# Four plain second-layer products instead of two ahead of a pair's outputs, and a later landing time told to a planner

## The chip, the core and the metric

The kernel runs on one core of one Trainium2 chip. The metric is device time in microseconds (us) of one execution, taken as the median of the runs. Five engines work beside each other, each through its own list of instructions in order: PE (matrix products), DVE, ACT and POOL (elementwise work) and SP, which here only issues DMA transfers. They wait for each other through semaphores.

## The reference, cut to what matters

Two blocks follow each other. The first is a chunked state-space scan over 4 sequences of 768 tokens with 8 heads of width 32 and a state of 16:

```
for each chunk:
    L = exp(cum_i - cum_j), lower triangle          # decays inside the chunk
    y = (C B^T * L) x  +  exp(cum) * (C state)      # outputs
    state = exp(cum_last) * state + sum_j exp(cum_last - cum_j) B_j x_j
```

The second is a mixture of 4 experts with a hidden layer of 1024, over the 3072 tokens (width 256) that the first block puts out; p is `domain_probs` divided by its row sum:

```
out = sum_e  p[:, e] * (max(x @ w1[e], 0) @ w2[e])
```

All of it is in float32.

## The kernel before, in words

**Chunks and pairs.** The kernel cuts the tokens into 24 chunks of 128, numbered so that chunks 0 to 3 open the four sequences, 4 to 7 are the second chunks, and so on. Chunks go in pairs. Of a pair, three steps matter here. `decays(c)` (L799) makes the decay triangle of a chunk: for chunks 3 to 5 by two running products on DVE (`scan`, L519) over a tile `ab` of 512 KB that a DMA (`load_decays`, L461, issued at L463) spreads over all partitions; chunk 2 is scanned from PSUM banks instead. There are two `ab` tiles, so chunk 3 and chunk 5 share `ab0`. `scores(cs)` (L844) is 16 small PE products (L502 in the trace) into four PSUM banks, each followed by one DVE multiplication with the triangle (L856) that gives the masked scores `MT`. `outputs(cs)` (L865) is 16 PE products for a pair (32 records of L546, and for chunks 4 and later also products with the carried state at L879); they read `MT`, so they need all four L856 of their pair. ACT then copies the results out (L894, L556), and `carry(c)` (L901) turns the new state on DVE (L910, L912).

**Experts.** A hidden piece of 256 columns is numbered `fb` 0 to 15. Tokens of the first pair go through pieces 0 to 3 plainly: `plain_first(fb)` (L1235) is four matrix instructions into a bank, and `gated` (L965, DVE instruction at L968) takes the bank through max(., 0) and the gate into an SBUF tile. The second layer of these four pieces is the list `own_` (L1390): eight products, two for each piece, all summed in one bank. Every product is two matrix instructions of 128x256 in the program (L933), and each of those is two records in the trace, so a product is four records. Products 1 and 2 need the gated tile of piece 0, 3 and 4 that of piece 1, and so on. All later pairs go through schemes with fewer products and more additions; `token_sums` (L1033, instruction L1043) makes sums of token tiles for them, `operands` (L989, L1024) sums of weights, on POOL or DVE, stored to DRAM at L1029. `twos_begun` (L1075) and the list `ones` (L1401) are first-layer products and two second-layer products of the first such group.

**The order on PE** is written by hand, as a list `line` (L1367 to L1505). Around the change it is: plain first layer of pieces 0 and 1, `scores([2, 3])`, plain first layer of pieces 2 and 3, the first `OWN` products of `own_`, `outputs([2, 3])`, the products of `own_` from `OWN` to `SCORED`, `scores([4, 5])`, the four products of `twos_begun` for both groups, then what is left of `ones` and `own_`, of which the last `LEFT` stand behind `outputs([4, 5])`, and then products on token sums (tiles `Y`).

```
    line.extend(own_[:OWN])
    outputs([2, 3])
...
    fill = own_[OWN:SCORED] + put(*[begun[two][0] for two in twos]) + ones + own_[SCORED:]
    line.extend(fill[:SCORED - OWN])
    scores([4, 5])
    line.extend(fill[SCORED - OWN:len(fill) - LEFT])
    outputs([4, 5])
    line.extend(fill[len(fill) - LEFT:])
```

**The order on the other engines** is made when the program is built, by `Plan.run` (L180): it walks through an assumed clock, in which every piece of work has an assumed duration, and gives an engine that is free the ready work with the earliest due time; due times come from the PE list. It also picks the PSUM bank or SBUF tile that a value lives in. [...] A tile that is filled ahead of the plan is handed over with the time at which the plan may count on it (`plan.taken`, L768 to L782); `now` is 13.2 (L745). That order is fixed in the program. On the chip an engine goes through its list, and an instruction that has to wait holds up everything behind it on that engine.

Of the kernel before, what the change touches and what calls it, by code (L numbers as in the profile page):

```python
# [33 lines left out]
LEAN = 4.0  # L34
EASY = 40.0
SCANNED = 6
SCORED, OWN, LEAD, LEFT = 5, 2, 5, 3
FILLED = 3
HORIZON, OPENING, LOADED = 26.0, 80.0, 1.0
ORDERS = (0, 1, 2, 3), (3, 1, 2, 0), (0, 1, 2, 3), (3, 1, 2, 0)  # L40
# [319 lines left out]
def kernel(  # L360
# [86 lines left out]
    st = {c: {} for c in range(NCH)}  # L447
# [294 lines left out]
    plan = Plan(homes)  # L742
    line = []
    B512, B256 = {"DVE": D512, "POOL": 1.3}, {"DVE": D256, "POOL": .72}
    now = 13.2  # L745
# [28 lines left out]
    for c, i in ((2, 2), (3, 3)):  # L774
        st[c]["xb"] = plan.taken("xb", i, now)
    st[2]["ctm"] = plan.taken("ctm", 0, now)
    st[3]["ab"] = plan.taken("ab", 0, now + 2)
    for c in range(2):
        st[c]["A"] = plan.taken("A", c, now)
    g0 = gates[0, 0] = plan.taken("gate", 0, now)  # L780
# [783 lines left out]
```

## Time and profile before

| what | us |
|---|---|
| runs before | 616.87, 616.92, 619.20; median 616.92 |
| profiled execution, first to last instruction (its span) | 615.3 |
| what lies around the span (median less span) | 1.6 |
| PE busy in the span | 605.7 (98%) |
| DVE, ACT, POOL busy | 489.5, 292.5, 157.6 |
| PE idle ahead of L546 (outputs of chunks 2 and 3) | 1.36 and 0.70 |

Times inside the execution are counted from its first instruction. The time of the profiled execution is its span and the start and end around it; set beside the median of the runs that rest is 1.6 us. "Busy" of PE counts a matrix instruction from its start to its modelled end, and neighbours overlap; so the spacing of two starts, not the duration of one, says how fast PE goes. The granted clock is the share of its full speed that PE was allowed in a stretch.

### The profile page before, as it was taken

What the parts mean: (1) busy time and instruction counts of PE and PEld (TensorE: products, weight loads), DVE (VectorE), ACT (ScalarE), POOL (GpSimd) and SP (SyncE); (2) the same over time, 40 slices, a digit from 0 to 9 for tenths busy, and PEclk for the clock granted to TensorE, in tenths of its full rate; (3) what the DMA queues carried; (4) which work ended last, traced back from release to release, by engine and by line L of the source; (5) the groups of instructions that cost most, each with busy time, mean ns of one, the idle gap of its engine ahead of it and who ended that gap; (6) DMA issues with size and microseconds to landing.
All of it is one profiled execution on the core that took longest, in us unless ns stands there. A gap on an engine that the chain in (4) does not pass through costs nothing.

```text
span 615.3 us, 10136 instructions
## 1 busy us (share of the span) xinstructions
PE 605.7 (98%) x3365; PEld 514.8 (84%) x3365; DVE 489.5 (80%) x854; ACT 292.5 (48%) x681; POOL 157.6 (26%) x238
## 2 busy tenths in 40 slices
PE   9899999999999999999999999999999999999997
PEld 5677878888888888888888888888888888888885
DVE  7879897998969895697978988386785979576775
ACT  4237646378651327877443333844444242434441
POOL 5536556636372000776500100210000000000000
PEclk9899999999999999999999999999999999999999
DMA  7737578676863429983442424964233232964001
GB/s 249 256 114 231 204 218 300 205 224 208 280 188 94 134 34 285 297 291 146 132 144 77 137 63 118 284 222 137 61 111 87 93 90 51 303 230 126 1 0 52
DMA packets 89060, 99.65 MB, mean 162 GB/s; under 512 B 27428, under 2 KB 58928, under 8 KB 89008
## 3 DMA queue, kind: packets, MB, share of 16 engines
q1 hardware_dynamic: 88852, 98.95, 51.4%
q8 instruction: 27, 0.44, 0.3%
q14 instruction: 25, 0.20, 0.1%
q10 hardware_dynamic: 156, 0.06, 0.0%
HBM read 78.80 MB, written 20.17 MB: 161 GB/s over the span
## 4 chain that ended last, share of the span: by engine, by line
PE 92%; DVE 2%; ACT 1%; issue 0%; DVEq 0%
PE bank L933 88%; PE bank L546 2%; PE bank L502 1%; PE bank L879 1%; DVE v L960 1%; DVE v L968 1%; ACT A L556 1%; DVE MT L856 0%; ACT v L894 0%; DVE bank L1071 0%; DVE v L1260 0%; PE bank L1325 0%; DVE v L1425 0%; ACT LT L894 0%; ACT v L1330 0%
## 5 line engine op out<-in xcount | busy, mean ns | idle before, releaser
L933 PE MATMUL bank<-v,w 128*128 128x256 f32 x1716 | 402.0, 381 | 1.1 <-DVE bank L1071 0.8
L933 PEld LDWEIGHTS bank<-v,w 128*128 128x128 f32 x1716 | 325.7, 191 | 50.0 <-issue 2.9
L933 PE MATMUL bank<-Y,w 128*128 128x256 f32 x692 | 177.3, 381 | 0.7 <-ACT LT L894 0.4
L933 PEld LDWEIGHTS bank<-Y,w 128*128 128x128 f32 x692 | 130.2, 190 | 21.9 <-issue 1.7
L1213 ACT COPY v<-bank 128x512 f32<-128x512 f32 x109 | 63.9, 586 | 177.5 <-PE bank L933 165.2
L968 DVE SCALAR_TENSOR_TENSOR v<-bank,gate 128x512 f32<-128x512 f32 x147 | 101.0, 688 | 39.6 <-PE bank L933 36.8
L960 DVE TENSOR_TENSOR v<-v,v 128x512 f32<-128x512 f32 x179 | 125.9, 720 | 2.1 <-ACT v L942 0.8
L1024 POOL TENSOR_TENSOR w<-w,w 128x256 f32<-128x256 f32 x94 | 72.1, 784 | 46.0 <-DVE v L960 13.8
L1071 DVE TENSOR_TENSOR bank<-bank,v 128x512 f32<-128x512 f32 x81 | 55.5, 696 | 35.2 <-PE bank L933 23.6
L942 ACT COPY v<-bank 128x512 f32<-128x512 f32 x97 | 56.7, 587 | 55.0 <-PE bank L933 46.7
L947 ACT COPY bank<-v 128x512 f32<-128x512 f32 x126 | 73.2, 594 | 10.8 <-DVE v L968 8.7
L526 ACT ACTIVATE MT<-ab,neg 128x128 f32<-128x128 f32 x144 | 46.9, 393 | 2.0 <-DMA ab<-cum_d 2.0
L933 PE MATMUL bank<-LT,w 128*128 128x256 f32 x168 | 42.6, 380 | 0.0
L531 POOL TENSOR_SCALAR_AFFINE_SELECT MT<-MT 128x512 f32<-128x512 f32 x36 | 23.0, 652 | 67.8 <-ACT MT L526 53.9
L933 PEld LDWEIGHTS bank<-LT,w 128*128 128x128 f32 x168 | 31.8, 190 | 4.6 <-DVE v L968 0.3
L1024 POOL TENSOR_TENSOR w<-w 128x256 f32<-128x256 f32 x32 | 24.2, 762 | 23.2 <-DVE Y L1043 9.0
L960 DVE TENSOR_TENSOR v<-bank,v 128x512 f32<-128x512 f32 x26 | 17.9, 689 | 11.7 <-PE bank L933 9.9
L1260 DVE TENSOR_TENSOR v<-v,v 128x256 f32<-128x256 f32 x58 | 22.9, 431 | 1.1 <-ACT v L1213 0.7
L856 DVE TENSOR_TENSOR MT<-bank,MT 128x512 f32<-128x512 f32 x36 | 22.7, 681 | 0.1
L968 DVE SCALAR_TENSOR_TENSOR v<-v,gate 128x512 f32<-128x512 f32 x26 | 19.7, 758 | 0.4
L1213 ACT COPY LT<-bank 128x512 f32<-128x512 f32 x12 | 7.0, 586 | 23.5 <-PE bank L933 23.5
L840 POOL TENSOR_TENSOR cts<-ctm,dec 128x256 f32<-128x256 f32 x20 | 14.5, 734 | 11.6 <-DVE v L960 5.1
(110 smaller groups left out, 322.1 us busy)
## 6 DMA issues: line engine op xcount, KB each, us to landing
w<-w_d SPq DMA_DIRECT2D x128, 256.0 KB
w_d<-w SPq DMA_DIRECT2D x64, 256.0 KB
w<-in_w_dram SPq DMA_DIRECT2D x40, 256.0 KB
ab<-cum_d SPq DMA_DIRECT2D x18, 512.0 KB
w<-in_w_dram SPq DMA_DIRECT2D x64, 128.0 KB
gate<-p_d SPq DMA_DIRECT2D x15, 384.0 KB
xb<-in_xbc_dram SPq DMA_DIRECT2D x17, 192.0 KB
out_dram<-v SPq DMA_DIRECT2D x144, 16.0 KB
```

Of the source, the lines that this page charges most:

```text
L526: nc.scalar.activation(out=MT[:, place(c, h), 0:P], in_=ab[:, h * P:h * P + P], func=AF.Exp, bias=neg[:, h % NT, NQ * real(c) + h // NT:NQ ...
L531: nc.gpsimd.affine_select(out=MT[:, h:h + n, 0:P], in_=MT[:, h:h + n, 0:P], compare_op=ALU.is_ge, fill=0.0, base=0, pattern=[[0, n], [1, P ...
L856: nc.vector.tensor_mul(to, g, LT0[:, js, h] if cs[0] < SCANNED else to)
L933: nc.tensor.matmul(out=o, lhsT=w[:, j], rhs=x if half is None else x[:, j], start=(start and j == 0), stop=(j == 1), skip_group_check=True)
L942: act(.5, lambda e: nc.scalar.copy(out=flat(v), in_=bank.t), reads=[bank], writes=[v])
L947: act(.54 if to - lo > FB else .32, lambda e: nc.scalar.copy(out=bank.t[:, lo:to], in_=flat(v)[:, lo:to]), reads=[v], writes=[bank])
L960: plan.add(engines, lambda e: (on(e).tensor_add if sign > 0 else on(e).tensor_sub)(flat(v), whole(x), whole(y)), reads=[x, y], writes=[v], ...
L968: dve(D512, lambda e: nc.vector.scalar_tensor_tensor(out=h.t, in0=whole(x).rearrange("p (j m) -> p j m", j=JJ), scalar=0.0, in1=g.t[:, 2 * ...
L1024: plan.add(B256, lambda e, r=r, x=x, y=y, sign=sign: (on(e).tensor_add if sign > 0 else on(e).tensor_sub)(view(r), view(x), view(y)), two= ...
L1071: dve(D512, lambda e: (nc.vector.tensor_add if sign > 0 else nc.vector.tensor_sub)(to.t, bank.t, whole(x)), reads=[x, bank], writes=[to])
L1213: act(.5, lambda e: nc.scalar.copy(out=flat(v), in_=bank.t), reads=[bank], writes=[v], hold=HOLD)
L1260: plan.add(engines, lambda e: (on(e).tensor_add if sign > 0 else on(e).tensor_sub)(o[1](), x[1](), y[1]()), reads=[v for v in vs if v is n ...
```

## The change

Two constants and one time are changed. `OWN` goes from 2 to 4 and `SCORED` from 5 to 7, so four products of `own_` stand ahead of `outputs([2, 3])`, still three between it and `scores([4, 5])`, and one, not three, is left over. As `LEFT` stays 3, the three products behind `outputs([4, 5])` are now the two of `ones` and the last of `own_`; before they were the last three of `own_`, and `ones` stood ahead of the outputs. The plan is told that the `ab` tile of chunk 3 is there at `now + 5.9`, which is 19.1 of its clock, instead of `now + 2`, which is 15.2. The number of instructions of each kind stays the same on every engine.

```
-SCORED, OWN, LEAD, LEFT = 5, 2, 5, 3
+SCORED, OWN, LEAD, LEFT = 7, 4, 5, 3
...
-    st[3]["ab"] = plan.taken("ab", 0, now + 2)
+    st[3]["ab"] = plan.taken("ab", 0, now + 5.9)
```

The planned orders of the two kernels, set beside each other by line, differ in these places and nowhere else but in the numbers of banks and tiles:

- PE: four matrix instructions (two products) go from behind the outputs of chunks 4 and 5 to ahead of the outputs of chunks 2 and 3, and two products of `ones` take their old place.
- DVE: before `L968 (piece 0), L519, L968 (piece 1), L519, L856, L968 (2), L856, L856, L968 (3), L856`; after `L968 (0), L968 (1), L519, L519, L968 (2), L856, L968 (3), L856, L856, L856`. Behind the scan of chunk 5 the four L856 of chunks 4 and 5 stand together, then the two L968 for `ones`; before, the two L968 stood in the middle. The carries of chunks 4 and 5 (two L910 and two L912) go some 25 instructions later, and four single instructions L968, L1043 and L1071 change places with a neighbour.
- POOL: the L540 of chunk 3 goes behind two sums of weights (L1024). ACT: L1217 goes behind the copies of chunks 4 and 5; two exponentials (L526) change places with a copy.
- SP: the fourth weight load (L477, 256 KB) of a group of four goes ahead of the second load of `ab0` (L463, 512 KB, for chunk 5); three stores (L1029) go one to two places up.

## The prediction

> **What bounds the kernel now.** I read the page first: PE is busy for 605.7 of 615.3 us, and the chain that ended last is 92% PE. So only the 9.6 us in which PE stands still, and stretches in which it runs slowly, can be won. The waits of PE, longest first, say where it stands still:
>
> ```profile
> engine line waited for: us in total, times, longest us
> PE bank L546 <- POOL w L1024: 1.4, 1, 1.4
> ...
> PE bank L933 <- DVE bank L1071: 0.8, 1, 0.8
> ...
> PE bank L546 <- DVE MT L856: 0.7, 1, 0.7
> ...
> PE bank L933 <- DVE v L968: 0.3, 1, 0.3
> ```
>
> Two of these, 1.36 + 0.70 = 2.06 us, are the outputs of chunks 2 and 3. POOL in the first line is misleading: the last POOL result needed was long there; L546 at 24.98 came 0.15 after the end of a DVE L856 (24.83), and the order says that it waits for that one. The busy times by stretch add a second cost; the columns are busy time (and count) of PE, PEld, DVE, ACT and POOL, then the granted clock, DMA share and GB/s:
>
> ```profile
> 23.00:24.00 1.00, 0.62 (x3) 0.19 (x1) 1.00 (x3) 0.05 (x1) 1.00 (x3) 1.00 0.95 313
> 24.00:25.00 1.00, 0.02 (x1) 0.06 (x2) 1.00 (x3) 0.00 (x0) 1.00 (x3) 1.00 0.81 224
> 25.00:26.00 1.00, 0.38 (x2) 0.09 (x2) 1.00 (x2) 0.00 (x0) 1.00 (x2) 1.00 0.77 179
> ...
> 27.00:28.00 1.00, 1.00 (x12) 0.68 (x3) 1.00 (x2) 0.85 (x4) 0.86 (x1) 0.69 1.06 385
> 28.00:29.00 1.00, 1.00 (x4) 0.78 (x3) 1.00 (x2) 0.93 (x6) 0.00 (x0) 0.50 0.85 324
> 29.00:30.00 1.00, 1.00 (x4) 0.82 (x3) 1.00 (x2) 0.21 (x2) 0.76 (x1) 0.50 0.44 170
> 30.00:31.00 1.00, 1.00 (x4) 0.79 (x4) 1.00 (x2) 0.00 (x0) 0.00 (x0) 0.60 0.12 48
> ```
>
> From 27.4 to 30.8 PE is granted half its clock: 0.31 + 0.50 + 0.50 + 0.40 = 1.71 us lost, while it looks busy. Nowhere else inside the span is it lower, but for the last 0.8 us. DVE, whose timeline I read last, is what PE waited for, and it had itself stood still for a DMA:
>
> ```profile
> 16.56 0.67 DVE L968 SCALAR_TENSOR_TENSOR v<-bank,gate 128x512 f32<-128x512 f32 x1
> 19.13 1.23 DVE L519 TENSOR_TENSOR_SCAN LT<-ab,ident 128x512 f32<-128x512 f32 x1 [1.90 <-DMA ab<-acut_d]
> 20.27 0.67 DVE L968 SCALAR_TENSOR_TENSOR v<-bank,gate 128x512 f32<-128x512 f32 x1
> ...
> 25.34 0.68 DVE L856 TENSOR_TENSOR MT<-bank,LT 128x512 f32<-128x512 f32 x1
> ```
>
> The decays of chunk 3 landed at 19.0; an L968 whose bank was full since 17.0 was queued behind the scan that waited for them.
>
> **The landing time.** It takes that L968 into the 1.90 us hole (17.2 to 17.8). The instructions between 19.13 and the last of the four L856 are then two L519 at a spacing of 1.14, two L968 and four L856 at 0.60 (starts at 19.13, 20.27, then every 0.60): the last L856 starts at 24.40 and ends at 25.1. Two POOL sums that wait for nothing now run up to 19.6, into the first scan; an L519 that met the end of a POOL sum at 20.85 took 1.39 instead of 1.23, so I add 0.2: end 25.3, against 26.02. L540 of chunk 3 ends near 22.7, early enough.
>
> **The two products.** The last record ahead of the outputs starts at 23.24. Eight records at 0.216 (full clock) are 1.73, a first record behind a wait costs 0.10 more (0.32 for 0.216, as at 32.74), and from the last record to the first L546 it is 0.31 (38.15 to 38.46): L546 at 25.4. DVE is done at 25.3. The stall is 0 to 0.3; I take none. The second tile that the new products read (piece 1) is ready at 17.8 and their weights were used by POOL at 24.8 at the latest, by increments of their semaphores at 14.9.
>
> From there PE has the same records as before, at full clock, up to the first product on token sums (42.86 before):
>
> - outputs of chunks 2 and 3: 1.12 (as 39.05 to 40.17), to 26.5
> - 12 records of products and the switch to L502: 2.79, to 29.3
> - scores of chunks 4 and 5: 1.08, to 30.4
> - 16 records of first-layer products with the switch: 3.73, to 34.1
> - L879 and L546 of chunks 4 and 5: 0.59 + 1.12, to 35.8
> - 12 records: 2.69, to 38.5
>
> 38.5 instead of 42.86 is **4.35 us earlier**: 2.06 of standing still, 1.71 of half clock, 0.4 in which two L546 ran alone, and small switches.
>
> Whether the clock comes back with the stall is the largest choice. In the row, 2.06 us of idle PE between 23.6 and 26.1 are followed by half clock for 3.41 us; idle times of 0.33 (at 50.4) and 0.80 (at 76.5) are not. I take it that the clock stays full. [...]
>
> **What is late next.** (a) The second load of `ab0` goes behind a 256 KB load on SP's queue. Before, DVE did not wait for it at 30.05; DMA is silent from 31 on; the increments of its queue end at 28.8, those of the load that passes it at 29.4. DVE now comes to it at 28.9 to 29.3 (25.4 and the 3.9 us from 26.11 to 30.05, less up to 0.4 by which a POOL sum stretched an L519 there). It is there between 28.8 and 31; I take 29.5, so DVE waits 0.2 to 0.6. From that scan to the end of the fourth L856 it is 2.25 + 0.40 + 3 x 0.60 + 0.68 = 5.1 us (spacings from 30.05, 32.29 and 23.55): 34.6. PE asks for it at 34.7. No stall at 29.5, 0.4 at 30.05, 1.4 at 31. (b) The two L968 for `ones` end at 35.2 and 35.8; their products start at 35.8 and 36.7. (c) The token sums start 0.47 after the outputs end and give the first `Y` needed 1.3 later; PE reaches it 2.7 after the outputs, as before. Queued behind DVE's wait in (a) are just these. (d) ACT's copies out of bank 5 (L894, L556) start about 0.5 us earlier and end by 28.6, before the scores at 29.3 overwrite it; before, that margin was 2.4.
>
> **Keeping the gain.** Behind 48.8 DVE stands still for only 1.51 + 0.31 + 0.19 + 0.10 us up to 92, so it must move up as well. In what lies before 48.8 it idled for 1.62, 0.17, 1.62, 0.27, 0.78 and 0.49, each time for PE or ACT: that is 4.95, which pays for 4.35. Beyond that point the orders are the same, and of the waits that the changed kernel has in addition none beyond 51 us had under 1 us to spare in the trace of before. Moving the carries takes four short instructions (0.2 to 0.25 each) out of DVE's list before the stall of 0.33 at 50.75, and the L968 that this stall waited for now stands one place (0.60) earlier; the next places with DVE just ahead of PE have 0.2 to spare, so this is worth 0 to 0.3. The carries then lie before the idle 1.51 at 66.6. I take 0.05. The stalls of 0.80 and 0.43 at 77 and 87 stay: both sides of them move together.
>
> The sum is -4.35 - 0.05 = **-4.4 us** on the profiled execution (span 610.9). The start is untouched, so I set it off from the median: 616.92 - 4.4 = **612.5**.
>
> **Rivals.**
>
> 1. The clock drops all the same, or dropped for another reason than the stall. Then 1.71 is not won: 614.2. For it: the drop begins 1.3 us after the stall has ended, and one event in one execution is all that shows the link. Against it: it is the only drop, and the stall the longest idle. 8%. [...]
> 2. The wait moves to the outputs of chunks 4 and 5. Between 30.05 and 31 for the load, or as much contention on DVE, PE stands 0.4 to 1.4: 612.9 to 613.9; with a half-clock window behind the longer ones up to 615.6. For it: DVE has no reserve between 25.3 and 34.6. Against it: the increments at 29.4. 10%.
> 3. The gain is given back where DVE is saturated (48.8 to 92), because POOL sums, stores or loads there do not move up with PE. DVE's idle 2.1 us are kept, the rest is lost: 614.8. For it: DVE is 92 to 100% busy there. Against it: POOL had idle stretches of 2.4 to 4.7 us before 46. 5%.
> 4. Slower: the load in (a) comes so late that the stall at the outputs of chunks 4 and 5, with a half-clock window of 1.71 behind it, is more than 4.4. That decides from 32.3 on; at 33 the stall is 3.4 and the time 616.92 - 4.4 + 5.1 = 617.6. Against it: the same transfers were over by 31 before. 2%.
>
> That the planner might not obey is no case: the built order shows the L968 ahead of the scan.
>
> **How the numbers follow.** The forecast has 75%, from 611.8 (the stalls at 50 and 77 shrink too) to 613.4 (0.3 and 0.5 of stalls at the two outputs). About 0.5% (3.1 us, a time of 613.84) is what a measurement of this kernel tells from no change. The forecast is below that, rival 2 mostly, rivals 1 and 3 above: faster 0.82, same 0.16, slower 0.02. The range for 8 in 10 takes in the half-known stalls and rival 1: 611.5 to 614.4.
>
> **What would show it.** Right: no idle of PE over 0.3 ahead of either L546; granted clock 1.00 from 24 to 34; the first product on `Y` at 38.5; the L519 of chunk 3 still begins at 19.1, with two L968 ahead of it. Wrong: a wait of L546 for L856 at 34 to 36, or a DVE wait for `ab` beyond 30 (rival 2); a clock below 1 with no idle before it (rival 1); the first `Y` product in time but larger stalls at L1071 and L968 between 50 and 92 (rival 3).

## The result and the profile after

The changed kernel takes 612.60 us (median of 9 runs, 612.37 to 613.25). In the same measurement the kernel before takes 615.59 us (9 runs, 614.59 to 619.20, the three shown ahead of the prediction among them). The ratio is 0.9953 with a 95% interval of 0.9937 to 0.9970: 0.47% faster, between 0.30% and 0.63%. A second measurement gave 612.48 against 614.96, ratio 0.9956 (0.9941 to 0.9971). The predicted time was 612.5; the gain is smaller than the predicted 4.4, because the kernel before is mostly faster than the 616.92 from which the prediction set off. Its executions fall into two groups, most around 614.9 and some 1.7 us or more above, and the difference between the groups is what most of the experiments are about. Where the text below speaks of the higher group, it means the runs in which the clock was halved for a while.

The profiled execution of the changed kernel has a span of 610.9 (612.72 timed). The waits of PE, longest first:

```profile
engine line waited for: us in total, times, longest us
PE bank L684 <- PEq L1556: 0.8, 1, 0.8
PE bank L1325 <- DVE v L1260: 0.7, 1, 0.7
PE bank L933 <- DVE bank L1071: 0.7, 1, 0.7
PE bank L933 <- ACT LT L894: 0.4, 1, 0.4
PE bank L502 <- ACT p_sb L647: 0.4, 1, 0.4
```

Both L546 waits, 1.36 and 0.70 before, are gone from the list, and so is the 0.33 of L933 for L968. The busy times by stretch (PE, PEld, DVE, ACT, POOL, then granted clock, DMA share, GB/s) show what became of the clock:

```profile
24.00:25.00 1.00, 0.99 (x6) 0.38 (x4) 1.00 (x2) 0.00 (x0) 1.00 (x3) 1.00 0.91 266
25.00:26.00 1.00, 0.90 (x28) 0.81 (x30) 0.91 (x2) 0.06 (x1) 0.56 (x1) 1.00 0.98 253
...
27.00:28.00 1.00, 1.00 (x6) 0.87 (x6) 1.00 (x3) 0.92 (x7) 0.10 (x1) 1.00 1.05 412
28.00:29.00 1.00, 1.00 (x6) 0.68 (x4) 0.95 (x2) 0.33 (x2) 0.67 (x1) 1.00 0.86 337
```

PE is idle for 0.01 + 0.10 us in the first two rows instead of 2.06 in all, and the granted clock is 1.00 in each row, where before it was 0.69 and 0.50 in the last two. PE's timeline (start, length, and how many records stand together) answers the prediction's table:

```profile
24.68 1.69 PE L546 MATMUL bank<-MT,xb 128*32 128x144 f32 x32
...
29.09 1.15 PE L502 MATMUL bank<-ctm,xb 32*128 32x256 f32 x16
...
34.48 1.19 PE L546 MATMUL bank<-MT,xb 128*32 128x144 f32 x32
...
38.45 2.75 PE L933 MATMUL bank<-Y,w 128*128 128x256 f32 x11
```

The outputs of chunks 2 and 3, the scores of chunks 4 and 5, the outputs of these and the first product on token sums follow each other without a wait that the list shows. The last of them starts at 38.45; forecast were 38.5, and before it was 42.86. DVE's timeline shows the new order and the two waits for `ab`:

```profile
15.90 1.26 DVE L968 SCALAR_TENSOR_TENSOR v<-bank,gate 128x512 f32<-128x512 f32 x2
19.22 2.34 DVE L519 TENSOR_TENSOR_SCAN LT<-ab,ident 128x512 f32<-128x512 f32 x2 [2.06 <-DMA ab<-acut_d]
...
23.26 1.88 DVE L856 TENSOR_TENSOR MT<-bank,LT 128x512 f32<-128x512 f32 x3
...
29.28 2.34 DVE L519 TENSOR_TENSOR_SCAN LT<-ab,ident 128x512 f32<-128x512 f32 x2 [0.33 <-DMA ab<-acut_d]
...
31.85 2.48 DVE L856 TENSOR_TENSOR MT<-bank,LT 128x512 f32<-128x512 f32 x4
```

Both L968 stand ahead of the scan, the last L856 of chunks 2 and 3 ends at 23.26 + 1.88 = 25.14, and the second load of `ab0` lands at 29.28, 0.33 after DVE could have begun. Its four L856 end at 31.85 + 2.48 = 34.33, and PE's outputs of chunks 4 and 5 did not have to wait.

### The profile page after: what moved, and what is told of

Read it like the earlier page. It is cut to its first block, busy times and chain, and to the rows that moved or that the text cites. A ratio compares the mean times of both kernels' runs of the same rounds, so it can differ in the third digit from the quotient of the medians.

```text
span 610.9 us, 10142 instructions
## 1 busy us (share of the span) xinstructions
PE 603.7 (99%) x3365; PEld 513.6 (84%) x3365; DVE 489.8 (80%) x854; ACT 292.9 (48%) x681; POOL 158.8 (26%) x238
## 4 chain that ended last, share of the span: by engine, by line
PE 92%; DVE 2%; ACT 1%; issue 0%; DVEq 0%
PE bank L933 88%; PE bank L546 2%; PE bank L502 1%; PE bank L879 1%; ACT A L556 1%; DVE v L968 1%; DVE v L960 0%; DVE MT L856 0%; ACT v L894 0%; DVE bank L1071 0%; DVE v L1260 0%; PE bank L1325 0%; DVE v L1425 0%; ACT LT L894 0%; ACT v L1330 0%
## 5 line engine op out<-in xcount | busy, mean ns | idle before, releaser
L933 PE MATMUL bank<-v,w 128*128 128x256 f32 x1676 | 394.8, 380 | 0.8 <-DVE bank L1071 0.7
L933 PEld LDWEIGHTS bank<-v,w 128*128 128x128 f32 x1676 | 316.9, 190 | 48.2 <-issue 2.2
L933 PE MATMUL bank<-Y,w 128*128 128x256 f32 x692 | 177.6, 381 | 0.7 <-ACT LT L894 0.4
L1213 ACT COPY v<-bank 128x512 f32<-128x512 f32 x109 | 64.0, 587 | 178.5 <-PE bank L933 166.2
L933 PEld LDWEIGHTS bank<-Y,w 128*128 128x128 f32 x692 | 130.2, 190 | 22.4 <-issue 2.0
L968 DVE SCALAR_TENSOR_TENSOR v<-bank,gate 128x512 f32<-128x512 f32 x149 | 102.3, 688 | 42.6 <-PE bank L933 39.7
L1071 DVE TENSOR_TENSOR bank<-bank,v 128x512 f32<-128x512 f32 x84 | 57.4, 696 | 35.7 <-PE bank L933 23.4
L942 ACT COPY v<-bank 128x512 f32<-128x512 f32 x100 | 58.6, 587 | 54.0 <-PE bank L933 45.0
L1024 POOL TENSOR_TENSOR w<-w,w 128x256 f32<-128x256 f32 x94 | 73.1, 794 | 42.5 <-DVE v L960 14.5
L933 PE MATMUL bank<-LT,w 128*128 128x256 f32 x208 | 52.7, 379 | 0.0
L526 ACT ACTIVATE MT<-ab,neg 128x128 f32<-128x128 f32 x144 | 47.1, 396 | 2.1 <-DMA ab<-cum_d 2.1
L933 PEld LDWEIGHTS bank<-LT,w 128*128 128x128 f32 x208 | 39.4, 190 | 5.3
L1024 POOL TENSOR_TENSOR w<-w 128x256 f32<-128x256 f32 x32 | 24.3, 763 | 18.8 <-DVE Y L1043 7.7
L856 DVE TENSOR_TENSOR MT<-bank,MT 128x512 f32<-128x512 f32 x36 | 22.7, 681 | 0.1
L1260 DVE TENSOR_TENSOR v<-v,v 128x256 f32<-128x256 f32 x55 | 21.1, 422 | 1.0 <-ACT v L1213 0.7
L960 POOL TENSOR_TENSOR v<-v,v 128x512 f32<-128x512 f32 x6 | 7.7, 1277 | 49.7 <-DVE v L960 49.7
L968 DVE SCALAR_TENSOR_TENSOR v<-v,gate 128x512 f32<-128x512 f32 x26 | 19.8, 763 | 0.4
L495 ACT ACTIVATE ctm<-xb,tmask 128x128 f32<-128x128 f32 x48 | 15.8, 395 | 3.8 <-DMA xb<-in_xbc_dram 3.7
```

The costliest lines, as they stand in the source:

```text
L526: nc.scalar.activation(out=MT[:, place(c, h), 0:P], in_=ab[:, h * P:h * P + P], func=AF.Exp, bias=neg[:, h % NT, NQ * real(c) + h // NT:NQ ...
L856: nc.vector.tensor_mul(to, g, LT0[:, js, h] if cs[0] < SCANNED else to)
L933: nc.tensor.matmul(out=o, lhsT=w[:, j], rhs=x if half is None else x[:, j], start=(start and j == 0), stop=(j == 1), skip_group_check=True)
L942: act(.5, lambda e: nc.scalar.copy(out=flat(v), in_=bank.t), reads=[bank], writes=[v])
L960: plan.add(engines, lambda e: (on(e).tensor_add if sign > 0 else on(e).tensor_sub)(flat(v), whole(x), whole(y)), reads=[x, y], writes=[v], ...
L968: dve(D512, lambda e: nc.vector.scalar_tensor_tensor(out=h.t, in0=whole(x).rearrange("p (j m) -> p j m", j=JJ), scalar=0.0, in1=g.t[:, 2 * ...
```

## The experiments

Two theories were set against each other. **The stall theory** (that of the prediction): the idle time ahead of L546 is the cost, it also brings the half clock, and both parts of the change are needed to remove it. **The rival**: the clock drops on its own, or the gain comes from one part only, the other being decoration. Times are medians; the ratio is to the kernel before on the same chip with its 95% interval, and it is not the plain quotient of the two medians (0.9951 in the first measurement).

| run | us | ratio | runs in the higher group |
|---|---|---|---|
| kernel before, three measurements | 614.86, 615.06, 614.96 | | 13 of 80 |
| e1_before, the same once more | 615.07 | 1.0004 (0.9992 to 1.0016) | 3 of 12 |
| e2_time, landing time alone | 614.59 | 0.9991 (0.9981 to 1.0001) | 0 of 12 |
| e3_own, two products alone | 613.17 | 0.9969 (0.9959 to 0.9978) | 0 of 12 |
| e4_filled, stall filled with idle work | 614.61 | 0.9994 (0.9982 to 1.0006) | 0 of 12 |
| e5_early, before with an earlier load | 614.85 | 0.9984 (0.9970 to 0.9997) | 0 of 12 |
| e6_own3, one product and landing time | 614.32 | 0.9982 (0.9972 to 0.9992) | 0 of 12 |
| e7_own5, three products and landing time | 613.01 | 0.9956 (0.9941 to 0.9970) | 0 of 6 |
| e8_both, the change with an earlier load | 613.67 | 0.9970 (0.9956 to 0.9983) | 0 of 8 |
| e9_after, the changed kernel once more | 612.48 | 0.9956 (0.9941 to 0.9971) | 0 of 9 |
| e10_own1, before with one product fewer | 617.21 | 1.0026 (1.0009 to 1.0044) | 7 of 12 |

A run is counted as higher where its mean granted clock is 0.997 or less. Those of the kernel before lie at 616.60 and above, and its others at 615.99 and below. The nine runs of the kernel before in the first measurement are not in the count, as their clock is not on record; four of them lie at 616.87 and above. In the versions with a shorter or a filled stall (the changed kernel with 18 runs and e2 to e8 with 74) none of 92 runs is higher; in their profiled executions the longest wait of PE in the first 60 us is 1.31.

**e1_before: the kernel before, unchanged.** There is no edit.

> The kernel before once more, unchanged, to see its spread. [...] Rival: the half clock comes in every execution and the spread has another origin; then every execution has a clock of about 0.997 and the times differ without it.

Measured: 615.07, nine runs from 614.45 to 615.43 with a mean clock of 0.999 or 1.0 and three from 616.69 to 616.94 with 0.996. The profiled execution belongs to the nine. Its waits of PE:

```profile
PE bank L546 <- POOL w L1024: 1.7, 1, 1.7
...
PE bank L546 <- DVE MT L856: 0.7, 1, 0.7
```

and its stretches:

```profile
24.00:25.00 1.00, 0.23 (x2) 0.14 (x2) 1.00 (x3) 0.00 (x0) 1.00 (x2) 1.00 0.75 219
25.00:26.00 1.00, 0.30 (x6) 0.12 (x8) 0.91 (x3) 0.00 (x0) 1.00 (x3) 1.00 0.78 212
...
27.00:28.00 1.00, 1.00 (x8) 0.90 (x6) 1.00 (x2) 0.84 (x4) 0.66 (x1) 1.00 1.03 384
```

The same stall, even 0.3 longer, and no half clock behind it: 1.00 in each row. So the stall does not bring the half clock each time: the times fall on two values. Here the first product on `Y` starts at 40.97, and against this execution the change wins 40.97 - 38.45 = 2.52, not 4.4.

Why one execution is hit and another not can only be estimated, from the times at which the clock changes in the traces. In each, it becomes full at some time between 3.7 and 6.9 after the span's start (before the first recorded change the rows by stretch print 1.00, but two L684 records start 0.80 apart at 5.26 in before, and the same two 0.43 apart at 4.59 in the changed kernel, whose clock is full from 3.74). In before it is full for 20.480 us from 6.909, half for 3.413 from 27.389, and full again for 583.679; in the changed kernel it is full for 607.572 from 3.744, to just past the end of the span. These are 6, 1, 171 and 178 times the 3.413 of the half clock, to within 0.02 of one. So each execution is divided here into stretches of 3.413, counted from the time at which its clock became full. That the clock goes by such stretches, and where they lie in an execution with no later change, is an estimate of the author's from these four lengths. The idle time of PE (no matrix instruction running) in the stretches around a stall, added up from the trace, with two stretches at the end of a span, where PE has done its last work:

| execution | stretch (estimate) | idle in it | clock behind it |
|---|---|---|---|
| before | 23.98 to 27.39 | 1.70 | half clock |
| e10_own1 | 21.04 to 24.46 | 2.26 | half clock |
| e1_before | 21.15 to 24.56 | 1.47 | full |
| e1_before | 24.56 to 27.98 | 0.91 | full |
| e5_early | 30.68 to 34.09 | 0.98 | full |
| after | 24.22 to 27.64 | 0.11 | full |
| e6_own3 | 607.13 to 610.54 | 1.67 | full |
| e4_filled | 607.50 to 610.91 | 1.82 | half clock |

By this estimate the stall of before fell nearly whole into one stretch, and in e1_before the end of one at 24.56 divided it. In the table the largest idle time with full clock behind it is 1.67 and the smallest with half clock behind it 1.70; as the ends of matrix instructions are modelled, these two are good to a few hundredths at best.

**e4_filled: the same order, with PE kept busy through the stall.** Two matrix instructions on constants (L684, four records) stand ahead of the outputs of chunks 2 and 3, in a bank that L546 overwrites; nothing is left out.

```
-            vs = {}
+            vs = {} if cs[0] != 2 else {None: [idle(ys[2].t) for _ in range(2)]}
```

> The kernel before with two matrix instructions of 128x512 on constants put into the stall ahead of the outputs of chunks 2 and 3, into the bank that those outputs then overwrite; they are work for nothing, 1.7 us of it, and all orders stay. Theory (a standstill of PE lowers the clock): PE still starts the outputs at 26.1, the clock is 1.00 from 24 to 31, the first product on token sums comes at 41.1 instead of 42.9, and the time is near 615.1 in all executions, within 1 us. [...]

Measured: 614.61, all twelve between 614.33 and 615.45, none in the higher group. PE's timeline:

```profile
23.45 1.89 PE L684 MATMUL bank<-const-float32-1.0 128*128 128x512 f32 x4
25.27 1.19 PE L546 MATMUL bank<-MT,xb 128*32 128x144 f32 x32
```

The work moved nowhere and nothing useful was added; only the idle time is gone, and with it the higher value. Twelve runs alone would be thin, since at 16 of 92 they hold no higher one by chance one time in ten; with the other versions it is none of 92. It saves what the higher runs cost and nothing of the lower ones (614.61 against 614.88, the median of the 76 lower runs of before). So the half clock is an effect of the stall, and rival 1 of the prediction falls. The stall itself still costs its time, since the useful products stand where they stood. The profiled execution is not the one that was expected, though: the load for chunk 3 came early, the last L856 ended at 24.53, and L546 had to wait for the idle work until 25.27 (expected 26.1). The first product on `Y` came at 40.37 instead of 41.1.

**e10_own1: a stall that begins sooner.** One product fewer ahead of the outputs.

```
-SCORED, OWN, LEAD, LEFT = 5, 2, 5, 3
+SCORED, OWN, LEAD, LEFT = 4, 1, 5, 3
```

> The kernel before with one product, not two, ahead of the outputs of chunks 2 and 3, so that PE stands still for about 0.9 us longer (some 2.9 instead of 2.06). [...] Rival (the drop has nothing to do with the length of the stall): the higher value again in about one of six.

Measured: five runs from 615.47 to 616.12, five from 617.12 to 617.63, and two at 618.99 and 619.46 with a mean clock of 0.994. The higher value comes in 7 of 12, not in about one of six. The stretches of the profiled execution:

```profile
22.00:23.00 1.00, 0.19 (x1) 0.00 (x0) 1.00 (x2) 0.14 (x1) 0.98 (x2) 1.00 0.91 295
23.00:24.00 1.00, 0.00 (x0) 0.00 (x0) 1.00 (x3) 0.00 (x0) 1.00 (x3) 1.00 0.93 299
24.00:25.00 1.00, 0.39 (x2) 0.18 (x2) 1.00 (x3) 0.00 (x0) 1.00 (x2) 0.73 0.98 281
25.00:26.00 1.00, 1.00 (x18) 0.76 (x20) 1.00 (x3) 0.00 (x0) 1.00 (x3) 0.50 0.86 266
```

and L546 on PE's timeline:

```profile
24.61 2.65 PE L546 MATMUL bank<-MT,xb 128*32 128x144 f32 x32 [2.41 <-POOL w L1024]
```

PE stands still from 22.2 to 24.6, and the half clock begins at 24.46, while it still stands: here there is no gap of 1.3 us between the stall and the drop as there was in before. By the estimate under e1_before that gap was the rest of the stretch that ends at 27.39. The stall became longer at its start, but not by 0.9 in all: the planner also put the last three L856 together, the last of them ends at 25.05 (25.82 in e1_before), and the idle time in the profiled execution is 2.41, against 2.38 in e1_before and 2.06 in before. What differs is that it is in one piece (against 1.68 and 0.70 in e1_before) and lies earlier. Which of the two makes the half clock come more often is not separated. What happens in the runs with 0.994 was not profiled; two half clocks at 1.71 lost would be 3.4 us, and they lie 3.0 and 3.4 above the middle of the lower group.

**e2_time and e3_own: each part alone.**

```
-    st[3]["ab"] = plan.taken("ab", 0, now + 2)
+    st[3]["ab"] = plan.taken("ab", 0, now + 5.9)
```

```
-SCORED, OWN, LEAD, LEFT = 5, 2, 5, 3
+SCORED, OWN, LEAD, LEFT = 7, 4, 5, 3
```

> The landing time alone (now + 5.9), OWN and SCORED as before. Theory: the L968 of piece 1 goes into DVE's hole and the last L856 of chunks 2 and 3 ends at 25.2 instead of 26.0; PE stands still for about 1.5 us instead of 2.4, so 0.8 us is won: 614.3 where the clock stays full and 616.1 where it drops. Rival (the landing time is what brings the gain): 612.6 as the full change.

> OWN 4 and SCORED 7 alone, the landing time as before. Theory: PE is ready for the outputs of chunks 2 and 3 at 25.4, DVE at 26.1 as before, so PE stands still for 0.7 us, the clock stays full, and the time is 0.7 us over the full change: 613.3. Rival (the landing time is what brings the gain): within 0.5 us of the kernel before, near 615.

Measured: the landing time alone 614.59, which can't be told from no change by its interval; the products alone 613.17, a gain of 0.31%. Neither has a higher run. In e2_time PE stops once for 1.10 ahead of L546. In e3_own it stops here:

```profile
25.08 0.43 PE L546 MATMUL bank<-MT,xb 128*32 128x144 f32 x2
26.12 1.18 PE L546 MATMUL bank<-MT,xb 128*32 128x144 f32 x30 [0.61 <-DVE MT L856]
```

The first two products find their masked scores, the other 30 wait for the last L856, which in the old order of DVE ends at 26.07. With the new order it ends at 25.14, so the landing time takes away the remaining 0.6. The first `Y` products start at 40.32 (landing time), 39.39 (products) and 38.45 (both), 0.65, 1.58 and 2.52 ahead of e1_before. In the medians, against the 614.88 of the lower runs of before, the two parts win 0.29 and 1.71, and both 2.30. So three quarters of the gain are the products; but only both together leave no wait of over 0.2 ahead of L546.

**e6_own3 and e7_own5: other numbers of products, with the landing time.** `SCORED, OWN` are 6, 3 and 8, 5.

> The changed kernel with OWN 3 and SCORED 6: one product moved instead of two. Theory: PE is ready at 24.5, DVE at 25.2, so 0.7 us of standstill stays and the clock stays full: 613.3, 0.7 over the change. If a short standstill already costs clock, 615.

> The changed kernel with OWN 5 and SCORED 8: three products moved. Theory: the outputs of chunks 2 and 3 already wait for nothing with two, so the third wins nothing: 612.3 to 612.9; the outputs of chunks 4 and 5 come at the same time as in the changed kernel, with DVE just ahead, so up to 0.5 can be lost there. Rival (each product moved is worth its 0.86 us): 611.8.

Measured: 614.32 and 613.01. With five products PE doesn't wait at L546 either, but a wait comes in a later place: the 0.33 for L968, gone with four, is back and larger (0.7 in the list of waits). It is 0.4 to 0.5 slower than four, 0.1 beyond the range expected. With three, the miss of 1.0 lies in two places. The first `Y` product starts at 39.59, 1.1 after that of the change: its own products ended only 0.2 sooner than the change's (this execution came to full clock at 6.4 and the changed kernel's at 3.7), L546 begins at 24.71 against 24.68, and four records more stand behind it. And the planner made another order farther back:

```profile
74.61 1.75 PE L933 MATMUL bank<-v,w 128*128 128x256 f32 x7 [1.06 <-POOL MT L531]
```

PE waits 1.06 for POOL at a place where the change waits 0.69 for DVE. So the time of a count is that of its whole planned order, and neighbours of the count chosen differ by such waits.

**e5_early and e8_both: the decays of chunk 3 loaded earlier,** ahead of four weight loads (L483) instead of behind them; e5 on the kernel before, e8 on the changed one.

```
+    load_decays(3, homes["ab"][0])
     for fb in range(4):
         load_w2(fb, homes["W"][4 + fb])
-    load_decays(3, homes["ab"][0])
```

> The kernel before with the load of chunk 3's decays issued ahead of the four second-layer weight loads instead of behind them; the orders of the computing engines stay. Theory (DVE's 1.90 us wait for this load is the root of PE's stall): the load lands by 16.5, the scan of chunk 3 starts at 17.2 instead of 19.1, the last L856 ends near 24.1 and PE, ready at 23.6, stands still for 0.5 us with a full clock: 613.2 to 613.4, almost the gain of the change without it. Rival (DVE's order and amount of work bind, not the load): 615 or more.

> The changed kernel with the early load of chunk 3's decays as well. Theory: DVE no longer holds PE at 25.2, which in the profiled execution of the changed kernel was 0.4 us late, but the outputs of chunks 4 and 5 then meet DVE's wait for the second load of the same tile: 612.2 to 612.7, at most 0.4 better. Rival (the load is worth the same in both kernels): 610.7.

Measured: 614.85 and 613.67. Both miss: e5 hardly gains, and e8 is 1.1 slower than the change alone. The load itself did what was meant: the scan of chunk 3 starts at 17.15 and 17.24 without the wait. But everything behind it on SP's queue came later, because the load's source was not there yet. It reads `acut_d`, which a store of SP, issued at 6.51 in e8_both, writes, and SP waits for that store with the whole queue behind it (us in total, times, longest us):

```profile
SPq L463 <- DMA acut_d<-v: 1.9, 1, 1.9
```

In the old place the four weight loads fill this time. SP's issues of the weight loads and of the loads for chunks 4 and 5 in the changed kernel:

```profile
8.31 2.85 SPq L483 DMA_DIRECT2D w<-in_w_dram  x4
...
16.30 1.12 SPq L463 DMA_DIRECT2D ab<-acut_d  x1
...
23.43 0.41 SPq L463 DMA_DIRECT2D ab<-acut_d  x1
```

and in e8_both:

```profile
10.77 1.97 SPq L483 DMA_DIRECT2D w<-in_w_dram  x4
...
19.80 0.33 SPq L463 DMA_DIRECT2D ab<-acut_d  x1
...
24.66 0.41 SPq L463 DMA_DIRECT2D ab<-acut_d  x1
```

The weight loads begin 2.46 later and the load for chunk 5 is issued 1.23 later. In e5_early the same wait for the store is 2.3. A second wait of SP in e8_both, 1.9 ahead of a token load (L459), is put down to the landing of a weight load. In e8_both it ends a wait of DVE, which ends one of PE:

```profile
30.53 2.34 DVE L519 TENSOR_TENSOR_SCAN LT<-ab,ident 128x512 f32<-128x512 f32 x2 [2.09 <-DMA ab<-acut_d]
```

```profile
34.53 1.14 PE L879 MATMUL bank<-cts,S 32*32 32x256 f32 x16 [0.95 <-DVE MT L856]
```

This is rival 2 of the prediction, brought about on purpose: the load lands at 30.5 instead of 29.3, the four L856 end 5.05 later, and PE stands 0.95 at the outputs of chunks 4 and 5; the 16 records of L879 behind that wait then take 1.07 instead of 0.59 up to the first L546, which starts 0.02 after the last L856 has ended. The time is 1.1 above the changed kernel's. In e5_early the same lateness (DVE waits 1.53 for `ab`, until 29.92) delays an L968 that stands behind the scan, and PE loses 1.31 of the 1.7 it had won:

```profile
34.42 1.99 PE L933 MATMUL bank<-v,w 128*128 128x256 f32 x8 [1.31 <-DVE v L968]
```

**e9_after: the changed kernel again.** There is no edit.

> The changed kernel once more, for more of its executions beside those of the kernel before on one chip. Theory (its stall is gone, so no half-clock window can fall on it): every execution between 612.3 and 613.4, none 1.5 us or more above the rest, and 2.3 to 3.0 us below the lower group of the kernel before; the kernel before shows a second value some 1.7 us higher in about one execution in six. Rival (half clock strikes wherever a window happens to fall, whatever PE does): the changed kernel shows a value 1.7 higher in about one execution in six too.

Measured: nine runs between 612.09 and 612.85, two of them up to 0.2 below the range expected, beside 20 of the kernel before, 16 of them from 613.61 to 615.97 and four from 616.98 to 617.67. In the profiled execution the first product on `Y` starts at 38.38, and DVE does not wait for the second load of `ab0` (28.94). With the first nine that is none higher of 18 for the change, against 16 of 92 for the kernel before. The median of the 18 is 612.58, that of the 76 lower runs of before 614.88: **2.3 us** is what the change saves where the clock is full, and about 2 us more in each run that the half clock hits. No version tried was faster than the changed kernel.

## Why the prediction came out as it did, step by step

**The landing time** (last L856 at 25.3): right, 25.14. Both L968 went into the hole, which lasted until 19.22. The 0.2 added for POOL did not come (the two scans took 2.34), and the scan began 0.1 later than in before. It is shown by e3_own that without this step 0.6 of stall stays.

**The two products** (L546 at 25.4, no stall): the start was 24.68, earlier than forecast, because this execution reached its full clock 3.2 us sooner than the one the sum was made against; the prediction took the clock to be full up to 27.4. In e9_after, with full clock from 4.93, L546 starts at 25.14, and in e7_own5, with full clock from 6.86 (6.91 in before) and one product (0.86) more, at 26.13, which is 25.27 without it. In the profiled execution of the changed kernel DVE's last L856 kept the third L546 until 25.19. The rows from there came 0.2 ahead of the forecast up to 35.60, and the last 12 records took 2.85 instead of 2.69 (2.69 in e9_after): 38.45 for 38.5, so 0.2 of that agreement is a small cancelling.

**The clock** is the term that was mis-sized. That the stall causes the drop is shown by the counts: 16 of 92 runs of before, 7 of 12 with a stall in one piece (e10_own1), and none of 92 in the versions in which it is shorter or filled, the 12 of e4_filled among them. But "1.71 of half clock" was taken as a cost of every execution of before, because the one profiled shows it. It is a cost of 16 executions of 92. At full clock the prediction's own table gives 4.35 - 1.71 = 2.64, and the measurements give 2.52 (first `Y` product against e1_before), 2.43 (last matrix instruction, 609.48 against 607.05) and 2.30 (medians). The predicted time was right all the same, since the 616.92 it was set off from had the half clock in it too: the three runs shown, 616.87, 616.92 and 619.20, all lie in the higher group, which on later measurements holds one in six. The base was 1.7 to 2 too high and the gain by as much too large, both for the same reason, so they cancel: the sum goes from an execution with the half clock to one without. What was wrong is the gain over the usual execution of before. The chance of 0.82 for a gain of over 0.5% suffered from it: 4.4 is 0.7%, and the measured 0.47% and 0.44% lie just below that bound, with intervals on both sides of it.

**What is late next.** (a) Right in size: DVE waited 0.33 for the second load (forecast 0.2 to 0.6, landing 29.28 for 29.5), and from there to the fourth L856 it was 5.05 (forecast 5.1). PE did not wait; e8_both shows that 1.25 us more cost a stall of 0.95 (by the prediction's table, 0.4 at 30.05 and 1.4 at 31, it would be 0.9). (b), (c) and (d) gave no stall in the list of waits.

**Keeping the gain.** Right: from the first `Y` product to the last matrix instruction it is 568.52 in before and 568.60 in the changed kernel. The stall of 0.33 at 50.75 was to be worth 0.05. It is gone as a wait of that name, and the 32nd record behind the first `Y` product comes at 7.55 instead of 7.89; but the 40th comes at 9.72 in both. DVE sets the pace there (a record of PE starts at 47.20, right behind an L968 that ends at 47.14), as rival 3 says of this stretch, and the win is back at nothing eight records later. The stall of 0.80 at 77 became 0.69 and that at 87 stayed 0.44. The sum of these is +0.08, not -0.05.

**Of the rivals,** 1 fell by e4_filled and by 92 executions with the stall shortened or filled and without a drop, 2 did not happen but has its place and price shown in e8_both, 3 is true of 0.3 us and not of the gain, and 4 was far: the load would have had to land 3 us later than it did.

What stays open: why runs with a mean clock of 0.994 exist, and whether the one piece of the stall or its earlier place made the drop more frequent in e10_own1. That the load for chunk 5 is late in e8_both because SP had waited for the store of `acut_d` is read from SP's waits and issues; it was not tried with the weight loads kept ahead of that wait.

## What to carry to other kernels

Before a loss that one execution shows is charged to a kernel, ask whether each execution has it: the half clock behind the stall came in 16 of 92 runs of the kernel before, and the three runs from which the prediction set off all lie in that higher group. Fill a stall with work that has to be done anyway rather than with idle work: here idle work saved only the clock (614.61 against 614.88 in the lower runs of before), moved work the stall too (613.17 in e3_own). And an earlier transfer on a shared queue can be paid for by those behind it: in e8_both SP waited 1.9 for a source that was not written yet, and the weight loads behind began 2.46 later; look at what the queue waits for and at the next transfer that somebody waits for.

## What the runs showed of the hardware that was not expected

- A half clock can be a matter of chance: it came in 0 of 18 executions with 0.1 us of idle time, in 16 of 92 with 2.1 to 2.4 in two pieces, and in 7 of 12 with 2.4 in one piece (idle times of the profiled executions).
- The time at which PE reaches full clock at the start moves between 3.7 and 6.9 us after the first instruction, and with it the first 25 us by about 0.5 us (last product ahead of L546 in before: 23.24, in e1_before: 22.71). Where PE then waits for DVE, this vanishes in the stall. With the stretches of 3.413 counted back to the start (the author's estimate, as under e1_before), the clock of the twelve traces became full behind the first one with 0.51 us or less of idle time (0.33 to 3.74 in the changed kernel), and not behind one with 0.76 (0.08 to 3.50 in before); later it stayed full behind one with 1.67 (e6_own3).
- The landing of the same load differs by execution, with the same place in SP's queue (issued at 10.8 to 11.7): the scan of chunk 3 waited for it until 18.43 to 19.22 in eight executions, while in e4_filled and e7_own5 it began at 17.63 and 18.27 behind a wait for POOL, with the load already there.
